# Expert blocks sorted by token count with falling sizes, weights addressed by a register, and GpSimd products in halves, in an RWKV-5 + mixture-of-experts kernel

## The chip, the cores and the metric

The kernel runs on one core of a Trainium2 chip. The metric is device time of one execution in microseconds. The engines are TensorE (PE in the profile; its weight loads are PEld), VectorE (DVE), ScalarE (ACT), GpSimd (POOL) and SyncE (SP, which here only issues DMAs).

## The reference

Attention with a decaying state (batch 4, 8 heads, 768 tokens, head size 48) gives x; then each token goes through one of eight experts with a hidden size of 1024:

```python
for t in range(S):
    cur = einsum('bhd,bhe->bhde', u[None] * k_t, v_t)
    y[:, :, t] = einsum('bhd,bhde->bhe', r_t, state + cur)
    state = w[None, :, :, None] * state + einsum('bhd,bhe->bhde', k_t, v_t)
...
logits = einsum('bsd,de->bse', x, w_gate)              # x: 4 x 768 x 384
local_gate = sigmoid(x @ w_local)
for b in range(B):
    prev_e = -1
    for s in range(S):
        fresh_e = argmax(logits[b, s])
        e = fresh_e if s == 0 or local_gate[b, s] < 0.5 else prev_e
        prev_e = e
        p = softmax(logits[b, s])
        out[b, s] = p[e] * (relu(x[b, s] @ w1[e]) @ w2[e])
```

How many tokens an expert gets depends on the data. Counted from the reference with its fixed inputs, experts 0 to 7 get 417, 353, 336, 448, 376, 390, 329 and 423 tokens; of those, batches 0 and 1 send 212 to expert 0 and 171 to expert 1.

## The kernel before

**Attention** works on 16 items (a batch and a pair of heads), six chunks of 128 tokens each, as matmuls with decays folded into r and k. `Attention.run` writes the order of all engines out by hand; nothing is scheduled. In iteration n, SP loads item n+2 (`load`), GpSimd makes three products for item n+1 (`scale`: ke, pd, rw, L154 to L157), VectorE makes kw (`added`, L165), masks the scores (am, L212), multiplies own (L197) and adds up xT (L237). The two score matmuls of an iteration take PSUM banks from a ring of three, and the second gets its bank when xT of the item before has been written. After each batch its logits are made (lp, L259, and lq, L267) and x is written to DRAM.

**Router.** `Router` finds each token's expert and its slot (the place among the expert's tokens) by scans and one-hot matmuls, in two groups: batches 0 and 1 inside the attention's iterations 9 to 16 (`g` in `run` is 8), batches 2 and 3 inside the first expert units (`Experts.routing`, by step s). Slots are turned into a table of token numbers and of gates by `summed` (matmuls of one-hots), `copied` and `turned`. Each expert owns four columns of 128 slots.

**Experts.** Work runs in ten units of `Experts.run`. Units 0 and 1 take the first 192 slots (HEAD) of experts 0 and 1, which need only batches 0 and 1; units 2 and 3 take the rest of these two experts, 256 slots each; units 4 to 9 take experts 2 to 7 with 448 slots each (CAP). A unit gathers its tokens' rows of x with indirect DMAs from GpSimd's queue (`gather`), transposes them on PE (`turn`, etp, copied to exT), and makes eight times h = w1 x, a ReLU on ScalarE (hT) and y += w2 hT. `drain` copies y to yT, and `send`, one a step during the next unit, transposes 128 slots (otp), multiplies by the gate (yo) and scatters the rows to the output. Slots that hold no token are computed too. Weights of the next expert (w1t, w2t, 1.5 MB each) are fetched by SP into a pool of two buffers, opened when attention's memory has been released. If an expert has more tokens than slots, `over` is above 0 and a branch behind the experts computes everything again in a general way (`general_experts`, 31 blocks of 128).

Of the kernel before, what the change touches and what calls it, by code (L numbers as in the profile page):

```python
# [20 lines left out]
P = 128  # L21
# [13 lines left out]
CAP = 448  # L35
# [6 lines left out]
TAIL = 256  # L42

# [13 lines left out]
class Attention:  # L57
# [9 lines left out]
    def __init__(self, tc, st, rk_d, kv_d, vT_d, x_d, w_t, wp_d, mask, ident, lt):  # L67
# [5 lines left out]
        self.late = st.enter_context(tc.tile_pool(name="late", bufs=2))  # L73
        self.wp = self.late.tile([P, H, 32], F32, name="wp", bufs=1)
        self.sel = self.late.tile([P, E + 1], F32, name="sel", bufs=1)
# [68 lines left out]
    def scale(self, n):  # L144

        nc, t, pw = self.nc, self.items[n], self.pw
        t["ke"] = self.two.tile([P, NCH, 2 * DH], F32, name="ke")
        t["pd"] = self.two.tile([P, NCH, P], F32, name="pd")
        t["rw"] = self.three.tile([P, NCH, P], F32, name="rw")
        hp = t["hp"]  # L150
        if n == 0:
            nc.vector.tensor_mul(t["rw"], t["rT"], spread(pw[:, hp, :P], 1, NCH))
            nc.gpsimd.tensor_mul(t["pd"], t["rT"], t["kT"])
        nc.gpsimd.tensor_mul(t["ke"], t["k"], spread(self.endT[:, hp].rearrange("p i d -> p (i d)"), 1, NCH))  # L154
        if n:
            nc.gpsimd.tensor_mul(t["pd"], t["rT"], t["kT"])  # L156
            nc.gpsimd.tensor_mul(t["rw"], t["rT"], spread(pw[:, hp, :P], 1, NCH))  # L157
# [67 lines left out]
    def before(self, n):  # L225
        nc, t = self.nc, self.items[n]
        if t["hp"] == 0:
            self.xTs[t["b"]] = self.late.tile([P, H, C2 * P], F32, name="xT")
            self.xs[t["b"]] = self.late.tile([P, NCH, D], F32, name="x")
# [23 lines left out]
    def logits(self, b, banks):  # L253
        nc, xT = self.nc, self.xTs[b]
        self.lTs[b] = lT = self.late.tile([P, 2, C2 * P], F32, name="lT", bufs=1)
# [15 lines left out]
    def run(self, router):  # L271
# [9 lines left out]
        for n in range(M + 1):  # L281
            if n + 2 < M:
                self.load(n + 2)
            if n == 0:
# [9 lines left out]
            if n == M:  # L294
                router.turned(0, pair("tb")[0])
                router.head()
# [118 lines left out]
class Router:  # L415
# [7 lines left out]

    def __init__(self, tc, once, mpp, lt, mask, ident, gid, sid, gate, over):
# [4 lines left out]
        self.tok = once.tile([P, E * ST], F32, name="tok")  # L429
        self.tok1 = once.tile([P, E * ST], F32, name="tok1")  # L430
        self.gid0 = once.tile([P, EARLY * ST], I32, name="gid0")
        self.g = []
        for i, (b0, nb) in enumerate(GROUPS):
            c = nb * NCH
            g = dict(b0=b0, nb=nb, nc=c, z=slice(b0 * NCH, b0 * NCH + c))
            for name, shape, dt in (
                    ("mx", [P, c], F32), ("eq", [P, c, E], F32), ("k", [P, c], F32), ("key", [P, c], F32),
                    ("run", [c, P], F32), ("rn", [P, c], F32), ("go", [P, c], F32), ("inc", [P, c + 1], F32),
                    ("ei", [P, 3, c], I32), ("oh", [P, E, c], F32),
                    ("ext", [P, E, c + 1], F32), ("exc", [P, E, c + 1], F32), ("seg", [P, E, c + 1], F32),  # L440
                    ("pos", [P, E, c], F32), ("far", [P, EARLY, c], F32), ("r", [P, c], F32), ("si", [P, 3, c], I32),
                    ("eqv", [P, c, E * ST], F32), ("val", [P, c, E * ST], F32), ("ohq", [P, c, P], F32),
                    ("ex", [P, c, E], F32), ("sm", [P, c], F32), ("pe", [P, c], F32)):
                g[name] = once.tile(shape, dt, name=f"{name}{i}")
            self.g.append(g)
# [13 lines left out]
    def constants(self, part):  # L459
# [12 lines left out]
        else:  # L472
            for g in self.g:
                nc.gpsimd.memset(g["seg"], 1.0)
                nc.gpsimd.memset(g["seg"][:, :, 0:1], 0.0)

                nc.gpsimd.memset(g["go"], 1.0)
                nc.gpsimd.memset(g["go"].rearrange("p (b c) -> p b c", c=NCH)[:, :, NCH - 1:], 0.0)
                nc.gpsimd.memset(g["inc"][:, 0:1], 0.0)
            nc.gpsimd.memset(self.g[0]["ext"][:, :, 0:1], 0.0)  # L480

            self.lim = self.tl("lim", [1, E])
            nc.gpsimd.memset(self.lim, float(CAP))
            nc.gpsimd.memset(self.lim[:, :EARLY], float(CAP + TAIL - HEAD))

# [19 lines left out]
    def runs(self, i):  # L505

        g = self.g[i]
        self.nc.vector.tensor_tensor_scan(g["run"], g["kp"], g["seg"][:g["nc"], 0, 0:1].to_broadcast([g["nc"], P]), 0.0,
# [13 lines left out]
    def one_hot(self, i):  # L522

        nc, g = self.nc, self.g[i]
        nc.vector.tensor_tensor_scan(g["inc"][:, 1:], g["bc"], g["go"], 0.0, Alu.max, Alu.mult)
# [14 lines left out]
    def slots(self, i):  # L540
# [3 lines left out]
        nc.vector.tensor_tensor_scan(g["exc"].rearrange("p e c -> p (e c)"), g["seg"].rearrange("p e c -> p (e c)"),  # L544
                                     g["ext"].rearrange("p e c -> p (e c)"), 0.0, Alu.mult, Alu.add)
        nc.vector.tensor_tensor(g["pos"], g["exc"][:, :, :n], g["rk"].rearrange("p (e c) -> p e c", e=E), op=Alu.add)
        if i == 0:

            nc.vector.tensor_scalar(g["far"], g["pos"][:, :EARLY], float(HEAD), float(TAIL - HEAD), Alu.is_ge, Alu.mult)
            nc.vector.tensor_tensor(g["pos"][:, :EARLY], g["pos"][:, :EARLY], g["far"], op=Alu.add)  # L550
        nc.vector.tensor_tensor(g["pos"], g["pos"], g["oh"], op=Alu.mult)
        nc.vector.tensor_reduce(g["r"], g["pos"].rearrange("p e c -> p c e"), axis=AX.X, op=Alu.add)
# [3 lines left out]
        end = g["exc"][:, :, n:]  # L556
        if i == 0:
            base = self.g[1]["ext"][:, :, 0:1]
            nc.vector.tensor_copy(base, end)
            nc.vector.tensor_scalar(base[:, :EARLY], end[:, :EARLY], float(TAIL - HEAD), float(TAIL), Alu.add, Alu.max)  # L560
        else:
            big = self.tl("big", [1, E])
            nc.vector.tensor_tensor(big, end[0:1, :, 0], self.lim, op=Alu.is_gt)
            nc.vector.tensor_reduce(self.over, big, axis=AX.X, op=Alu.add)

    def columns(self, i):
# [3 lines left out]
        nc.vector.tensor_tensor(g["val"], g["eqv"], spread(self.t1[:, g["z"]], 2, E * ST), op=Alu.mult)  # L570
# [20 lines left out]
    def turned(self, what, bank):  # L591

        nc = self.nc
        nc.tensor.transpose(bank[:, :P], self.rows, self.ident)
        out = self.gate if what else self.tok
        nc.vector.tensor_reduce(out, bank[:, :P].rearrange("q (k j) -> q j k", k=4), axis=AX.X, op=Alu.add)

    def head(self):

        self.nc.vector.tensor_scalar(self.gid0, self.tok[:, :EARLY * ST], -1.0, 0.0, Alu.add, Alu.max)  # L600

    def tokens(self):
        nc = self.nc
        nc.vector.tensor_scalar(self.tok1, self.tok, -1.0, 0.0, Alu.add, Alu.max)
        nc.vector.tensor_scalar(self.gid, self.tok1, float(N - 1), None, Alu.min)
# [13 lines left out]

    def ends(self):  # L620
        nc = self.nc
        none = self.tl("none", [P, E * ST])
        nc.vector.tensor_scalar(none, self.tok, 0.0, float(4 * N), Alu.is_equal, Alu.mult)
        nc.vector.scalar_tensor_tensor(self.sid, self.tok, -1.0, none, Alu.add, Alu.add)
# [168 lines left out]
class Experts:  # L793
# [4 lines left out]
    def __init__(self, tc, st, x_d, w1, w2, out, ident, router):  # L798
        self.tc, self.nc = tc, tc.nc
        self.x_d, self.w1, self.w2, self.ident, self.router = x_d, w1, w2, ident, router  # L800

        self.outs = dram_disjoint_views(out, E * ST)

        def unit(e, first, slots):
# [358 lines left out]
```

## Time and profile before

| | |
|---|---|
| median of 3 timed runs | 475.46 us (474.88 to 477.63) |
| profiled execution | 480.13 us, span 478.3 us |
| attention | 0 to about 136 us |
| units 0 and 1 (192 slots) | about 144 to 183 us |
| units 2 and 3 (256 slots) | about 183 to 229 us |
| units 4 to 9 (448 slots) | about 229 to 459 us |
| mean granted TensorE clock | 0.968 |

A profile row of the timeline gives start, duration, engine, line, operation, output and inputs, shape, and in brackets the idle time of the engine before it with what ended it. Rows that follow each other without a gap are merged (x6 is six instructions, whose time is given together). A float32 matmul shows as two passes.

### The profile page before, as it was taken

What the parts mean: (1) busy time and instruction counts of PE and PEld (TensorE: products, weight loads), DVE (VectorE), ACT (ScalarE), POOL (GpSimd) and SP (SyncE); (2) the same over time, 40 slices, a digit from 0 to 9 for tenths busy, and PEclk for the clock granted to TensorE, in tenths of its full rate; (3) what the DMA queues carried; (4) which work ended last, traced back from release to release, by engine and by line L of the source; (5) the groups of instructions that cost most, each with busy time, mean ns of one, the idle gap of its engine ahead of it and who ended that gap; (6) DMA issues with size and microseconds to landing.
All of it is one profiled execution on the core that took longest, in us unless ns stands there. A gap on an engine that the chain in (4) does not pass through costs nothing.

```text
span 478.3 us, 8704 instructions
## 1 busy us (share of the span) xinstructions
PE 444.1 (93%) x3721; PEld 306.8 (64%) x3721; DVE 159.8 (33%) x266; ACT 78.5 (16%) x226; POOL 147.7 (31%) x142
## 2 busy tenths in 40 slices
PE   3999899969979999999999999999999999999970
PEld 1898897958859989888555555555555555555530
DVE  7597687894811622121101111111111121111030
ACT  2123223213212211111111111110111010110100
POOL 4989785744030021522021014024014002001020
PEclk9999999988978999999999999999999999999995
DMA  8978979752437120271710712612431250001001
GB/s 305 382 244 290 343 276 308 271 191 102 168 147 297 68 66 19 82 299 58 281 40 25 265 44 58 229 68 74 152 153 45 89 220 34 0 2 43 0 33 29
DMA packets 16911, 69.34 MB, mean 145 GB/s; under 512 B 2877, under 2 KB 6263, under 8 KB 14816
## 3 DMA queue, kind: packets, MB, share of 16 engines
q1 hardware_dynamic: 9600, 50.60, 29.1%
q0 software_dynamic: 3840, 10.23, 6.5%
q10 hardware_dynamic: 3424, 7.86, 4.3%
q8 instruction: 31, 0.51, 0.4%
q14 instruction: 16, 0.13, 0.1%
HBM read 59.25 MB, written 10.22 MB: 145 GB/s over the span
## 4 chain that ended last, share of the span: by engine, by line
issue 53%; PE 29%; POOL 11%; DVE 2%; another core or an unknown queue 1%; DMA 1%; POOLq 0%; ACT 0%; SPq 0%; DVEq 0%; ACTq 0%
POOL out_dram L896 6%; PE sc L210 6%; POOL xg L846 5%; PE yp L221 4%; PE tp L246 3%; PE T L172 3%; PE dp L193 2%; PE h L867 2%; PE y L878 2%; PE T L181 2%; PE yp L234 2%; PE lq L267 1%; PE lp L259 1%; DMA rk<-in_rk_dram 1%
## 5 line engine op out<-in xcount | busy, mean ns | idle before, releaser
L878 PE MATMUL y<-hT,w2t 128*128 128x448 f32 (+2 forms) x480 | 158.5, 466 | 1.1 <-ACT hT L870 1.1
L867 PE MATMUL h<-exT,w1t 128*128 128x448 f32 (+2 forms) x480 | 158.4, 470 | 0.0
L867 PEld LDWEIGHTS h<-exT,w1t 128*128 128x128 f32 x480 | 88.8, 194 | 50.2 <-issue 47.8
L878 PEld LDWEIGHTS y<-hT,w2t 128*128 128x128 f32 x480 | 86.3, 191 | 47.4 <-issue 43.5
L896 POOL DMA_INDIRECT out_dram<-yo,sid x32 | 31.4, 982 | 214.4 <-DVE yo L895 213.8
L870 ACT ACTIVATE hT<-h 128x448 f32<-128x448 f32 (+2 forms) x80 | 37.4, 468 | 241.8 <-PE h L867 241.8
L895 DVE TENSOR_SCALAR yo<-otp,gate 128x384 f32<-128x384 f32 (+1 forms) x32 | 19.5, 615 | 107.9 <-PE otp L893 107.7
L846 POOL DMA_INDIRECT xg<-x_d,gid x32 | 32.2, 1005 | 70.2 <-DVE ex L610 29.5
L860 DVE COPY exT<-etp 128x384 f32<-128x384 f32 (+1 forms) x32 | 16.2, 507 | 112.7 <-PE etp L859 112.7
L210 PE MATMUL sc<-rw,kw 48*64 48x128 f32 x768 | 32.9, 287 | 3.9 <-DVE xT L237 3.9
L154 POOL TENSOR_TENSOR ke<-kv,endT 128x576 f32<-128x576 f32 x16 | 24.6, 1539 | 20.4 <-PE T L172 9.5
L156 POOL TENSOR_TENSOR pd<-rk 128x768 f32<-128x768 f32 x15 | 28.0, 1868 | 9.0 <-issue 6.1
L210 PEld LDWEIGHTS sc<-rw,kw 48*64 48x64 f32 x768 | 28.1, 141 | 4.0 <-DVE xT L237 4.0
L212 DVE TENSOR_TENSOR am<-sc,mask 128x768 f32<-128x768 f32 x32 | 29.1, 948 | 2.9 <-PE sc L210 2.9
L181 PE MATMUL T<-S,wd 48*64 48x64 f32 x256 | 27.6, 236 | 0.6 <-ACT S L174 0.3
L157 POOL TENSOR_TENSOR rw<-rk,pw 128x768 f32<-128x768 f32 x15 | 26.6, 1772 | 0.0
L221 PE MATMUL yp<-am,kv 128*64 128x128 f32 x384 | 25.7, 284 | 0.8 <-issue 0.8
L181 PEld LDWEIGHTS T<-S,wd 48*64 48x64 f32 x256 | 22.0, 140 | 5.1 <-issue 2.7
L183 ACT COPY S<-T 128x64 f32<-128x64 f32 x64 | 13.6, 212 | 67.2 <-PE T L181 67.2
L237 DVE TENSOR_TENSOR xT<-yp,own 128x768 f32<-128x768 f32 x16 | 15.3, 956 | 24.4 <-PE yp L234 24.3
L221 PEld LDWEIGHTS yp<-am,kv 128*64 128x64 f32 x384 | 22.0, 143 | 1.3 <-issue 1.2
L165 DVE TENSOR_TENSOR kw<-rk,inv 128x768 f32<-128x768 f32 x16 | 22.6, 1410 | 0.1
(136 smaller groups left out, 300.4 us busy)
## 6 DMA issues: line engine op xcount, KB each, us to landing
rk<-in_rk_dram SPq DMA_DIRECT2D x16, 768.0 KB, 5.0
w1t<-in_w_dram SPq DMA_DIRECT2D x7, 1536.0 KB, 6.8
w2t<-in_w_dram SPq DMA_DIRECT2D x7, 1536.0 KB, 8.2
kv<-in_kv_dram SPq DMA_DIRECT2D x16, 584.0 KB, 6.1
vT<-in_vT_dram SPq DMA_DIRECT2D x16, 384.0 KB, 5.4
x_d<-x ACTq DMA_DIRECT2D x4, 1152.0 KB, 7.9
w1t<-in_w_dram ACTq DMA_DIRECT2D x1, 1536.0 KB, 7.8
w2t<-in_w_dram ACTq DMA_DIRECT2D x1, 1536.0 KB, 11.1
```

What stands on the lines that cost most here:

```text
L154: nc.gpsimd.tensor_mul(t["ke"], t["k"], spread(self.endT[:, hp].rearrange("p i d -> p (i d)"), 1, NCH))
L156: nc.gpsimd.tensor_mul(t["pd"], t["rT"], t["kT"])
L157: nc.gpsimd.tensor_mul(t["rw"], t["rT"], spread(pw[:, hp, :P], 1, NCH))
L181: nc.tensor.matmul(t["T"][h * DP:(h + 1) * DP, c], lhsT=self.wd[q, t["hp"]], rhs=t["S"][q, c - 1], start=False, stop=True, skip_group_chec ...
L210: nc.tensor.matmul(sc[z, h, c * P:(c + 1) * P], lhsT=t["kw"][q, 3 * g + c, z], rhs=t["rw"][q, 3 * g + c], start=True, stop=True)
L212: nc.vector.tensor_mul(t["am"][:, g], sc[:, :, :3 * P].rearrange("p h (c t) -> p h c t", t=P), spread(spread(self.mask, 1, 3), 1, 2))
L221: nc.tensor.matmul(t["y"][p * DP:(p + 1) * DP, h, c2 * P:(c2 + 1) * P], lhsT=t["v"][:, (2 * c + h) * DH:(2 * c + h) * DH + DP], rhs=t["am" ...
L846: self.nc.gpsimd.indirect_dma_start(out=xg[:n], out_offset=None, in_=self.x_d[:rows], in_offset=bass.IndirectOffsetOnAxis(ap=gid[:n, c:c + ...
L867: nc.tensor.matmul(h[:, :n], lhsT=u["w1"][:, m, kk, :], rhs=u["xT"][:, kk, :], start=(kk == 0), stop=(kk == DK - 1))
L870: nc.scalar.activation(u[m], h[:, :n], Act.Relu)
L878: nc.tensor.matmul(u["y"][d][:, :n], lhsT=u["w2"][:, m, d * P:(d + 1) * P], rhs=u[m], start=(m == 0), stop=(m == FK - 1))
L896: nc.gpsimd.indirect_dma_start(out=self.outs[c], out_offset=bass.IndirectOffsetOnAxis(ap=r.sid[:n, c:c + 1], axis=0), in_=yo[:n], in_offse ...
```

## The change

The last eight units are no longer tied to an expert. When all tokens are counted, VectorE ranks the experts by the tokens that are still to be done, the most first (`Router.blocks`, seven small operations at step 4, between pos and r), and unit 2 + b takes the expert of rank b with a fixed number of slots, `BLOCKS[b]`. The tail of experts 0 and 1 becomes such a block like the others, and their weights are fetched a second time. The expert's number is read by SP from `order` into a register, which addresses the weights. The tables of tokens and gates are permuted from experts to blocks by a product with the one-hot `of` and a sum (`rest`); units 0 and 1 have small tables of their own (`heads`). `exceeded` compares each expert's rest with its block's size.

```diff
-CAP = 448
+BLOCKS = (448, 424, 392, 376, 352, 336, 232, 192)
...
-        nc.gpsimd.tensor_mul(t["ke"], t["k"], spread(self.endT[:, hp].rearrange("p i d -> p (i d)"), 1, NCH))
+        for z in (slice(0, C2), slice(C2, NCH)):
+            nc.gpsimd.tensor_mul(t["ke"][:, z], t["k"][:, z], spread(self.endT[:, hp].rearrange("p i d -> p (i d)"), 1, C2))
         if n:
-            nc.gpsimd.tensor_mul(t["pd"], t["rT"], t["kT"])
-            nc.gpsimd.tensor_mul(t["rw"], t["rT"], spread(pw[:, hp, :P], 1, NCH))
+            for z in (slice(0, C2), slice(C2, NCH)):
+                nc.gpsimd.tensor_mul(t["pd"][:, z], t["rT"][:, z], t["kT"][:, z])
+            for z in (slice(0, C2), slice(C2, NCH)):
+                nc.gpsimd.tensor_mul(t["rw"][:, z], t["rT"][:, z], spread(pw[:, hp, :P], 1, C2))
...
             if n + 2 < M:
                 self.load(n + 2)
+            elif n + 2 == M:
+                fetch()
...
             if n == g + 4:
+                router.ranks(0)
+            if n == g + 5:
                 router.slots(0)
-            if n == g + 5:
                 router.columns(0)
-            if n in (g + 6, g + 7):
-                router.places(0, n - g - 6)
+            if n == g + 6:
+                router.numbers(0)
+                router.places(0, 0)
+            if n == g + 7:
+                router.places(0, 1)
...
+    def blocks(self):
+        nc, end = self.nc, self.g[1]["exc"][:, :, self.g[1]["nc"]]
...
+        nc.vector.scalar_tensor_tensor(self.c8, end, float(E), self.tie, Alu.mult, Alu.add)
+        nc.vector.tensor_tensor(gt, spread(self.c8, 1, E), spread(self.c8, 2, E), op=Alu.is_gt)
+        nc.vector.tensor_reduce(rank, gt, axis=AX.X, op=Alu.add)
+        nc.vector.tensor_tensor(self.of, spread(rank, 1, E), spread(self.ie, 2, E), op=Alu.is_equal)
...
+    def rest(self, table, out):
+        nc.vector.tensor_reduce(self.tok[:, EARLY:], table[:, EARLY:], axis=AX.X, op=Alu.add)
+        nc.vector.tensor_reduce(self.tok[:, :EARLY, :2], table[:, :EARLY, TAIL // P:], axis=AX.X, op=Alu.add)
...
+        nc.vector.tensor_tensor(self.by, spread(self.tok.rearrange("p e j -> p j e"), 1, E), spread(self.of, 2, ST), op=Alu.mult)
+        nc.vector.tensor_reduce(out.rearrange("p (b j) -> p b j", b=E), self.by, axis=AX.X, op=Alu.add)
...
-        self.units += [unit(e, TAIL // P, CAP - HEAD) for e in range(EARLY)]
-        self.units += [unit(e, 0, CAP) for e in range(EARLY, E)]
+        self.units += [unit(None, n, b * ST, r.gid, r.sid, r.gate) for b, n in enumerate(BLOCKS)]
...
+        self.wps = [st.enter_context(tc.tile_pool(name="wp0", bufs=1, reuse_waits="tile"))]
...
+            e = self.nc.values_load(self.router.order[0:1, i - EARLY:i - EARLY + 1], engines=[ET.SP], min_val=0, max_val=E - 1,
...
+            w1, w2 = [w[bass.ds(e, 1)].rearrange("o p x -> (o p) x") for w in (self.w1, self.w2)]
...
         if s == 4:
             r.counts(1, [bank("rk1"), bank("tt1")])
+            r.ranks(1)
+            r.blocks()
             r.slots(1)
             r.columns(1)
+            r.numbers(1)
...
+        if s == 5:
+            self.fetch(EARLY, self.nc.sync)
...
-        att.run(router)
+        att.run(router, lambda: ex.fetch(0, nc.sync))
         ex.open(st)
-        ex.fetch(0, nc.sync)
```

Three places show what moves. The first is VectorE in attention's iteration 12 (`n == g + 4`), from the product kw to xT; before, it held the whole slot arithmetic (exc, pos and far are ranks, r and si are slots):

```order
L165 TENSOR_TENSOR kw<-rk_160,inv 128x768
L544 SCALAR_TENSOR_TENSOR exc_100<-seg_101,ext_99 128x104
L546 TENSOR_TENSOR pos_102<-exc_100,rk 128x96
L549 TENSOR_SCALAR far_103<-pos_102 128x24
L550 TENSOR_TENSOR pos_102<-pos_102,far_103 128x24
L551 TENSOR_TENSOR pos_102<-pos_102,oh_98 128x96
L552 TENSOR_REDUCE r_104<-pos_102 128x12
L553 SCALAR_TENSOR_TENSOR si_105<-r_104,ei_97 128x12
L554 TENSOR_SCALAR si_105<-si_105 128x12
L555 TENSOR_SCALAR si_105<-si_105 128x12
L559 COPY ext_122<-exc_100 128x8
L560 TENSOR_SCALAR ext_122<-exc_100 128x2
```

After, on the same engine, r and si stand one iteration later, behind the next xT, own, am and kw:

```order
L585 TENSOR_TENSOR pos_104<-pos_104,oh_102 128x96
L243 TENSOR_TENSOR xT<-yp,own 128x768
L203 TENSOR_TENSOR own<-dp,vT_145 128x768
L218 TENSOR_TENSOR am<-sc,mask 128x768 x2
L171 TENSOR_TENSOR kw<-rk_140,inv 128x768
L614 TENSOR_REDUCE r_106<-pos_104 128x12
L615 SCALAR_TENSOR_TENSOR si_107<-r_106,ei_101 128x12
L616 TENSOR_SCALAR si_107<-si_107 128x12
L617 TENSOR_SCALAR si_107<-si_107 128x12
L622 TENSOR_TENSOR eqv_108<-si_107,ij_i 128x384
```

Four operations left the row ahead of xT. The second place is VectorE at the start of unit 1 (step 8), where the gather's token numbers (gid) are made ahead of the softmax (ex); before:

```order
L596 TENSOR_REDUCE tok<-tb_2307 128x32
L604 TENSOR_SCALAR tok_87<-tok 128x32
L605 TENSOR_SCALAR gid<-tok_87 128x32
L610 TENSOR_TENSOR ex_109<-lt,mx_89 128x96
L612 TENSOR_REDUCE sm_110<-ex_109 128x12
```

and after, with the permutation to blocks (by is the product with the one-hot):

```order
L659 TENSOR_REDUCE tok<-tb_2393 128x24
L660 TENSOR_REDUCE tok<-tb_2393 128x2x2
L663 TENSOR_TENSOR by<-tok,of 128x256
L664 TENSOR_REDUCE tok_2394<-by 128x32
L670 TENSOR_SCALAR at_2401<-tok_2394 128x32
L671 TENSOR_SCALAR gid<-at_2401 128x32
L700 TENSOR_TENSOR ex_111<-lt,mx_94 128x96
```

Three operations more stand ahead of ex, on which ScalarE's exponential and the ReLU behind it wait. The third place is SP's queue, from the last load of attention (vT) on; after the change:

```order
L142 DMA vT_145<-in_vT_dram 128x768
L924 DMA w1t<-in_w_dram 128x3072
L926 DMA w2t<-in_w_dram 128x3072
L920 TENSOR_LOAD order
L924 ISA
L924 DMA w1t<-in_w_dram 128x3072
L926 ISA
L926 DMA w2t<-in_w_dram 128x3072
```

The first pair goes to memory of its own and is not held back by attention's buffers any more; each later pair has a register load and two preparing instructions ahead of it. Unit 1's pair is still issued by ScalarE.

More of the change, by code (lines that the diff above doesn't have):

```diff
@@ L432, in __init__ @@
+        self.order = once.tile([1, E], I32, name="order")
         self.g = []
         for i, (b0, nb) in enumerate(GROUPS):
[L434 to L444, printed above, removed]
```

207 lines of the change are left out of this document (130 added, 77 removed).

## The prediction

> **What bounds the kernel now.** I read the page first, then the table by windows, the timeline of each stage, and the chain of waits for the attention stage.
>
> ```profile
> PE 444.1 (93%) x3721; PEld 306.8 (64%) x3721; DVE 159.8 (33%) x266; ACT 78.5 (16%) x226; POOL 147.7 (31%) x142
> ```
>
> TensorE is busy for 93% of the span, so a gain must shorten what PE does or one of its waits. The timeline shows what expert matmuls cost; a row holds three matmuls of two passes each.
>
> ```profile
> 170.46 1.14 PE L867 MATMUL h<-exT,w1t 128*128 128x192 f32 x6
> 171.43 1.14 PE L878 MATMUL y<-hT,w2t 128*128 128x192 f32 x6
> ...
> 243.38 2.42 PE L878 MATMUL y<-hT,w2t 128*128 128x448 f32 x6
> 245.63 2.42 PE L867 MATMUL h<-exT,w1t 128*128 128x448 f32 x6
> ...
> 262.61 0.33 SPq L831 DMA_DIRECT2D w1t<-in_w_dram  x1
> 301.52 0.33 SPq L831 DMA_DIRECT2D w1t<-in_w_dram  x1
> ```
>
> From start to start six passes take 0.97 us with 192 slots and 2.25 us with 448: 1.28 us for 256 slots, 5.0 ns a slot, with almost nothing fixed (192 x 5.0 ns is 0.96). A unit has 16 such groups, so a slot costs 80 ns. Two fetches stand 38.91 us apart, the length of one 448 unit: 16 x 2.25 = 36.0, and 2.9 for eight passes of three transposes, 0.36 each. From 183 us on PE is bound by slots alone.
>
> Before that there are two holes, each followed by a low granted clock. In the windows table the columns are busy us (instructions) of PE, PEld, DVE, ACT, POOL, then clock and DMA.
>
> ```profile
> 20.00:30.00 10.00, 10.00 (x238) 9.08 (x236) 7.95 (x9) 2.40 (x10) 10.00 (x7) 1.00 0.69 220
> 60.00:70.00 10.00, 10.00 (x244) 9.24 (x245) 7.86 (x9) 3.06 (x12) 8.24 (x6) 1.00 0.71 253
> 100.00:110.00 10.00, 6.15 (x79) 3.71 (x72) 8.72 (x12) 1.28 (x4) 3.02 (x2) 0.67 0.34 126
> 130.00:145.00 15.00, 12.07 (x115) 9.28 (x112) 4.22 (x13) 2.83 (x8) 4.18 (x4) 0.75 0.39 141
> ```
>
> **Blocks: the main term.** Slots over all units fall from 2 x 192 + 2 x 256 + 6 x 448 = 3584 to 2 x 192 + 2752 = 3136. 448 x 80 ns = **-35.8 us**. Units stay ten, so nothing fixed is added. Chunk passes inside the stream: gathers turned 30 before, 27 after; sends 28 before, 27 after (the last unit's are in the tail): 4 x 0.36 = **-1.4**. The partly filled chunks are bounded by nothing and a whole pass; I count whole ones.
>
> **Tail.** The last unit has 192 slots instead of 448.
>
> ```profile
> 183.47 0.68 DVE L886 COPY yT<-y 128x192 f32<-128x192 f32 x2
> 460.01 1.31 DVE L886 COPY yT<-y 128x448 f32<-128x448 f32 x2 [16.75 <-PE y L878]
> 462.64 0.98 POOL L896 DMA_INDIRECT out_dram<-yo,sid  x1 [18.18 <-DVE yo L895]
> 466.51 0.91 POOL L896 DMA_INDIRECT out_dram<-yo,sid  x1 [0.30 <-issue]
> ```
>
> Four sends stand 1.29 us apart and two remain: -2.6; the two drain copies on VectorE fall from 1.31 to 0.68: -0.6. **-3.2**.
>
> **Attention.** Its beat is the write of xT.
>
> ```profile
> 34.15 0.96 DVE L237 TENSOR_TENSOR xT<-yp,own 128x768 f32<-128x768 f32 x1 [0.42 <-PE yp L234]
> 40.23 0.96 DVE L237 TENSOR_TENSOR xT<-yp,own 128x768 f32<-128x768 f32 x1 [1.10 <-PE yp L234]
> 49.33 0.96 DVE L237 TENSOR_TENSOR xT<-yp,own 128x768 f32<-128x768 f32 x1 [3.76 <-PE yp L234]
> ...
> 92.56 0.95 DVE L237 TENSOR_TENSOR xT<-yp,own 128x768 f32<-128x768 f32 x1
> 99.42 0.32 DVE L552 TENSOR_REDUCE r<-pos 128x12 f32<-128x96 f32 x1
> 99.77 1.77 DVE L553 SCALAR_TENSOR_TENSOR si<-r,ei 128x12 int32<-128x12 f32 x1
> 103.31 0.95 DVE L237 TENSOR_TENSOR xT<-yp,own 128x768 f32<-128x768 f32 x1
> 114.88 0.96 DVE L237 TENSOR_TENSOR xT<-yp,own 128x768 f32<-128x768 f32 x1 [6.06 <-PE yp L234]
> ...
> 99.72 1.80 POOL L156 TENSOR_TENSOR pd<-rk 128x768 f32<-128x768 f32 x1 [0.89 <-POOL ke L154]
> ...
> 104.32 1.55 PE L210 MATMUL sc<-rw,kw 48*64 48x128 f32 x24 [3.85 <-DVE xT L237]
> ```
>
> A plain iteration takes 6.08 us, one with logits 9.10. The iteration with the slot arithmetic takes 10.75 (4.67 too long) and the next, with logits at the low clock, 11.57 (2.47 too long). From 99.42 to 103.04 VectorE is at r and si, and a 12-element operation lasts 1.77 us because GpSimd's pd runs beside it: both end within 0.03 us of each other. The change moves r and si behind the next kw, into the iteration whose xT has 3.76 us of idle time before it (row 49.33). So 3.6 us of stall go, and with them, likely, the low clock behind it (2.47). What is late next: about 1 us stays before xT (exc, far, pos). The product of numbers, now in one iteration with half of ohq, adds some 0.3 us there. **-5.8**, with ends -2.5 (clock stays low) and -7.1.
>
> GpSimd in halves: each of its three products an iteration becomes two instructions. What the cut costs isn't shown; I bound it by what a 768-element product holds beyond its elements: 1.80 us against 1.40 for the 576 of ke leaves some 0.15 at most, three times an iteration, so 0 to 0.4. At 8.24 us busy in 10, or 5.0 of 6.08, GpSimd has 1.1 us an iteration spare beside PE's work, so I cost it at 0; at 20 to 30 us it has none (10.00), and there every further 0.1 would be paid: see the rivals. Eight more small constants at about 48 us stand in the same slack.
>
> **First weights.** Fetched after the last load (about 105 us) instead of 120 and 129, when attention's memory came free. Nothing waited for them; the gain can only be at the passage to the experts.
>
> ```profile
> 128.88 0.33 SPq L833 DMA_DIRECT2D w2t<-in_w_dram  x1
> 131.83 1.26 POOL L846 DMA_INDIRECT xg<-x_d,gid  x1 [12.59 <-DVE gid L600]
> 135.02 0.85 PE L259 MATMUL lp<-xT,wp 64*32 64x384 f32 x8 [0.33 <-DVE xT L237]
> 137.79 0.86 ACT L262 COPY lT<-lp 128x384 f32<-128x384 f32 x2 [6.17 <-remote]
> 138.32 1.41 PE L859 MATMUL etp<-ident,xg 128*128 128x128 f32 x6 [2.46 <-ACT lT L262]
> 139.88 2.73 PE L267 MATMUL lq<-sel,lT 128*128 128x9 f32 x12
> 143.77 4.05 PE L867 MATMUL h<-exT,w1t 128*128 128x192 f32 x12
> ...
> 74.32 1.44 PE lq L267 x12
> ```
>
> PE is idle for 2.46 us although lp had ended at 135.87; ScalarE's copy started 1.9 us after that, for a reason the trace calls remote. In the same microseconds the 1.5 MB of w2t and the head gathers are under way. Behind the hole the clock is low: lq 2.73 instead of 1.44, twelve passes of h 4.05 instead of 1.94, and about 1.0 in the transposes between: 4.4 us. If the gathers no longer meet w2t, 1.6 of the hole and the 4.4 go; if the unknown releaser is something else, nothing goes. Between 0 and 6.0 I take **-5.0**, nearer to the rows of earlier batches, where lT follows lp at once.
>
> **What is added in units 0 and 1.**
>
> ```profile
> 165.42 0.29 DVE L596 TENSOR_REDUCE tok<-tb 128x32 f32<-128x128 f32 x1 [0.72 <-PE tb L594]
> 168.82 0.28 ACT L611 ACTIVATE ex<-ex 128x96 f32<-128x96 f32 x1 [2.21 <-DVE ex L610]
> 169.38 1.24 PE L878 MATMUL y<-hT,w2t 128*128 128x192 f32 x6 [1.07 <-ACT hT L870]
> 183.60 2.75 PE L867 MATMUL h<-exT,w1t 128*128 128x256 f32 x12
> ...
> L109 DVE TENSOR_TENSOR pw<-pw 128x256 f32<-128x256 f32 x1 | 0.4, 424 | 0.0
> ```
>
> At the start of unit 1 PE already waits 1.07 us for a ReLU queued on ScalarE behind two exponentials, which wait for VectorE. VectorE now does six rows for the gather's numbers instead of three, among them a product of 128x256 (0.42 by the last row) and its sum (0.29 to 0.6; I take 0.45): +1.1 us, so PE waits 2.2. At step 14 some 13 small rows more, about 2.9 us, stand ahead of two exT copies; the next unit's first h comes 0.7 later through two more transposed chunks, so 0.5 remains (0 to 1.5). At step 4 seven rows (1.3 us) stand before ohq, which had 1.1 us in hand: 0.2. **+1.8**.
>
> **Weights by a register.** The load of the number and a preparing instruction stand on SP ahead of each pair of fetches, which wait anyway for the unit before to release its buffer.
>
> ```profile
> w1t<-in_w_dram SPq DMA_DIRECT2D x7, 1536.0 KB, 6.8
> w2t<-in_w_dram SPq DMA_DIRECT2D x7, 1536.0 KB, 8.2
> ```
>
> The last number is the median us to landing, so a pair lands within 15 us even if one follows the other; the shortest cover is a unit of 192 slots, 15.5 us and its transposes, for unit 2, and w2 is needed later than w1. I cost it at 0; the bound above is a few us once.
>
> **Sum.** -35.8 - 1.4 - 3.2 - 5.8 - 5.0 + 1.8 = -49.4. The profiled execution took 480.13 us (span 478.3 and 1.8 around it): 430.7. The median of the timed runs is 4.67 us lower. If they save it in the low-clock stretches, which go anyway, none of it carries over; otherwise all. Half of it gives **428.4 us**.
>
> **Rivals.**
> - The passage stays as it is: 5 more, about 433. For it: the unnamed releaser. Against: w2t's traffic is gone from there.
> - A new low-clock stretch in unit 1, after the 2.2 us wait: the window of 0.67 above holds some 7 us at half clock, 3.5 to 4.5 more, 432.5. For it: a hole of 2.46 us was followed by the low clock. Against: the 1.07 us wait was not. The Trainium skill ("TensorE: Matmul & The Clock Gate", Part 1) puts the fall behind a whole idle window of about 3.4 us. By that rule this rival would add nothing; the row at 138.32 shows less idle time before a low clock, so I leave the rival its chance.
> - GpSimd becomes the bound in attention. It gives way to kw between two halves: 5.0 us of work, 0.3 for the cuts and up to 0.95 of waiting are 6.25 against 6.08, 0.2 x 14 iterations = 2.4 more, 431. The Trainium skill ("SBUF — State Buffer", Who interferes with whom) says that whichever of the two starts first holds the shared ports for the whole instruction; the ends at 101.5 agree, and by it a half stops VectorE for half as long but can be stopped as often again.
> - Weights come late, where an address from a register costs more than a fixed one: past 15 us a pair, unit 2 waits, then the last units: 5 to 15 more, 438.
> - Slower: a block overflows. Counting the reference's choices, 448, 423, 390, 376, 336, 329, 225 and 182 tokens remain for blocks of 448, 424, 392, 376, 352, 336, 232 and 192. Two fit with nothing to spare. If one token more falls into such an expert on the chip, the branch behind the experts computes everything again in 31 blocks of 128: 31 x 128 x 80 ns = 317 us more, some 745. Against it: expert 3 had exactly 448 of 448 before too, and the page ends without the branch.
>
> **Chances.** Forecast (within 424 to 431.5) 0.58; passage stays 0.16; low clock in unit 1 0.10; GpSimd 0.05; weights 0.06; overflow 0.03; 0.02 for a smaller time than all. The range of 421 to 438 reaches from all gains at their ends (about 422) to two of the small rivals together. About 0.5%, 2.4 us, is what a measurement can tell: every case but overflow is faster by far more. Faster 0.96, same 0.01, slower 0.03.
>
> **What would show it.** After: rows of y with 424, 392, 376, 352, 336, 232 slots, each 5.0 ns a slot; no PE wait for xT over 1.2 us near 100 us; clock 1.00 in that window and at the passage; y waiting for hT some 2.2 us in unit 1; SP's fetches landing before their units. A floor under the small matmuls, a PE wait for DMA at a unit's start, or rows behind the branch would make it wrong.

## The result and the profile after

The changed kernel's median is 428.0 us (425.7 to 431.1, 4 runs) against 475.17 for the kernel before beside it: a ratio of 0.901, 95% interval 0.893 to 0.909. Profiled it took 429.32 us, span 427.4. It was run again on a chip where the kernel before takes 478.55 us: 434.75, a ratio of 0.907 (0.905 to 0.910). The gain is 44 to 47 us.

The page's busy times and two groups of instructions (busy us, mean ns of one | idle us before, and what ended most of it):

```profile
PE 401.2 (94%) x3703; PEld 299.7 (70%) x3703; DVE 155.1 (36%) x282; ACT 75.1 (18%) x226; POOL 154.4 (36%) x190
...
L967 PE MATMUL y<-hT,w2t 128*128 128x192 f32 (+7 forms) x480 | 140.7, 430 | 2.2 <-ACT hT L959 2.2
L956 PE MATMUL h<-exT,w1t 128*128 128x192 f32 (+7 forms) x480 | 140.5, 433 | 0.1
```

TensorE does 43 us less and is as full as before. Of the 960 passes of the expert matmuls only one waits noticeably, one of y in unit 1 (2.2 us); none waits for weights from the register-addressed fetches. The timeline of the changed kernel shows the blocks, six passes a row:

```profile
199.94 2.42 PE L967 MATMUL y<-hT,w2t 128*128 128x448 f32 x6
...
228.44 2.30 PE L967 MATMUL y<-hT,w2t 128*128 128x424 f32 x6
...
255.86 2.14 PE L967 MATMUL y<-hT,w2t 128*128 128x392 f32 x6
...
305.75 2.06 PE L967 MATMUL y<-hT,w2t 128*128 128x376 f32 x6
...
329.70 1.94 PE L967 MATMUL y<-hT,w2t 128*128 128x352 f32 x6
...
352.08 1.86 PE L967 MATMUL y<-hT,w2t 128*128 128x336 f32 x6
...
389.83 1.34 PE L967 MATMUL y<-hT,w2t 128*128 128x232 f32 x6
...
404.25 1.14 PE L967 MATMUL y<-hT,w2t 128*128 128x192 f32 x6
```

From 448 to 192 slots, 1.28 us go for 256 slots: 5.0 ns a slot, without a floor down to 192 slots. Where the time went by stage, from the starts of the xT writes (items counted from 0), of each unit's first h, and the end of the last y; two profiles of each kernel, the second ones (before_again, after_again) both from one chip:

| stage, us | before | before_again | after | after_again |
|---|---|---|---|---|
| start to xT of item 10 | 92.56 | 92.90 | 91.87 | 92.78 |
| two iterations with slot arithmetic and logits | 22.32 | 21.26 | 15.90 | 16.49 |
| three more, to the last xT | 19.12 | 19.10 | 18.76 | 19.31 |
| passage: last xT to first h | 9.77 | 8.68 | 6.71 | 10.15 |
| unit 0 | 20.36 | 20.64 | 20.70 | 19.73 |
| unit 1 | 19.47 | 19.47 | 21.70 | 23.38 |
| units 2 to 9 | 277.06 | 277.07 | 238.53 | 238.53 |
| from the last y to the end | 17.65 | 17.64 | 13.23 | 13.15 |
| span | 478.31 | 476.76 | 427.39 | 433.51 |

The stream repeats to 0.01 us. What differs most between the two profiles of the changed kernel is the passage (3.4 us) and unit 1 (1.7), the two places where TensorE waits; no other stage of either kernel differs by more than 1.1. At the passage the first profile of the changed kernel seemed to show the forecast:

```profile
127.99 1.02 POOL L935 DMA_INDIRECT xg<-x_d,gid  x1 [0.30 <-issue]
128.44 0.86 ACT L268 COPY lT<-lp 128x384 f32<-128x384 f32 x2 [3.60 <-PE lp L265]
...
128.97 0.98 PE L948 MATMUL etp<-ident,xg 128*128 128x128 f32 x6 [0.58 <-ACT lT L268]
...
130.17 1.91 PE L273 MATMUL lq<-sel,lT 128*128 128x9 f32 x12 [0.21 <-DVE exT L949]
...
133.24 4.05 PE L956 MATMUL h<-exT,w1t 128*128 128x192 f32 x12
```

lT follows lp at once and the hole is 0.58 instead of 2.46. Yet lq takes 1.91 where 1.44 was its time in an earlier batch (2.73 at the passage before the change), and h 4.05 as before: a low clock stayed. In unit 1 the wait is the one forecast:

```profile
159.49 0.25 DVE L700 TENSOR_TENSOR ex<-lt,mx 128x96 f32<-128x96 f32 x1
159.78 0.28 ACT L701 ACTIVATE ex<-ex 128x96 f32<-128x96 f32 x1 [2.21 <-DVE ex L700]
159.97 0.53 ACT L959 ACTIVATE hT<-h 128x192 f32<-128x192 f32 x2
...
160.33 1.24 PE L967 MATMUL y<-hT,w2t 128*128 128x192 f32 x6 [2.21 <-ACT hT L959]
```

VectorE feeds the exponential, ScalarE does the ReLU (hT) behind it, and y waits 2.21 us.

### The profile page after: what moved, and what is told of

It reads as the page before. It is cut to its first block, busy times and chain, and to the rows that moved or that the text cites. A ratio compares the mean times of both kernels' runs of the same rounds, so it can differ in the third digit from the quotient of the medians.

```text
span 427.4 us, 8781 instructions
## 1 busy us (share of the span) xinstructions
PE 401.2 (94%) x3703; PEld 299.7 (70%) x3703; DVE 155.1 (36%) x282; ACT 75.1 (18%) x226; POOL 154.4 (36%) x190
## 4 chain that ended last, share of the span: by engine, by line
PE 87%; DVE 5%; DMA 2%; issue 2%; POOL 1%; SPq 1%; ACT 0%; DVEq 0%; ACTq 0%
PE h L956 30%; PE y L967 29%; PE sc L216 5%; PE yp L227 5%; PE tp L252 3%; PE T L178 2%; PE otp L982 2%; PE etp L948 2%; PE dp L199 2%; DMA kv<-in_kv_dram 2%; PE yp L240 2%; PE lp L265 1%; PE lq L273 1%; PE T L187 1%; DVE am L218 1%
## 5 line engine op out<-in xcount | busy, mean ns | idle before, releaser
L967 PE MATMUL y<-hT,w2t 128*128 128x192 f32 (+7 forms) x480 | 140.7, 430 | 2.2 <-ACT hT L959 2.2
L956 PE MATMUL h<-exT,w1t 128*128 128x192 f32 (+7 forms) x480 | 140.5, 433 | 0.1
L985 POOL DMA_INDIRECT out_dram<-yo,sid x29 | 28.7, 989 | 194.2 <-DVE yo L984 193.9
L959 ACT ACTIVATE hT<-h 128x192 f32<-128x192 f32 (+7 forms) x80 | 34.4, 431 | 211.9 <-PE h L956 211.9
L949 DVE COPY exT<-etp 128x384 f32<-128x384 f32 (+7 forms) x29 | 14.1, 493 | 103.9 <-PE etp L948 103.9
L984 DVE TENSOR_SCALAR yo<-otp,gate 128x384 f32<-128x384 f32 (+7 forms) x29 | 17.8, 615 | 91.5 <-PE otp L982 91.5
L935 POOL DMA_INDIRECT xg<-x_d,gid x29 | 29.6, 1022 | 52.5 <-DVE ex L700 27.1
L161 POOL TENSOR_TENSOR pd<-rk 128x384 f32<-128x384 f32 x30 | 32.3, 1098 | 6.2 <-issue 5.2
L163 POOL TENSOR_TENSOR rw<-rk,pw 128x384 f32<-128x384 f32 x30 | 33.1, 1123 | 0.0
L158 POOL TENSOR_TENSOR ke<-kv,endT 128x288 f32<-128x288 f32 x32 | 25.5, 818 | 5.3 <-DMA kv<-in_kv_dram 2.4
## 6 DMA issues: line engine op xcount, KB each, us to landing
x_d<-x ACTq DMA_DIRECT2D x4, 1152.0 KB, 10.6
```

Of the source, the lines that this page charges most:

```text
L158: nc.gpsimd.tensor_mul(t["ke"][:, z], t["k"][:, z], spread(self.endT[:, hp].rearrange("p i d -> p (i d)"), 1, C2))
L161: nc.gpsimd.tensor_mul(t["pd"][:, z], t["rT"][:, z], t["kT"][:, z])
L163: nc.gpsimd.tensor_mul(t["rw"][:, z], t["rT"][:, z], spread(pw[:, hp, :P], 1, C2))
L935: self.nc.gpsimd.indirect_dma_start(out=xg[:n], out_offset=None, in_=self.x_d[:rows], in_offset=bass.IndirectOffsetOnAxis(ap=u["gid"][:n, ...
L956: nc.tensor.matmul(h[:, :n], lhsT=u["w1"][:, m, kk, :], rhs=u["xT"][:, kk, :], start=(kk == 0), stop=(kk == DK - 1))
L959: nc.scalar.activation(u[m], h[:, :n], Act.Relu)
```

## The experiments

They went to four chips: e_flat, e_whole, e_back and e_late to one (the kernel before takes 475.6 there), b_split, e_w2, e_fill and e_fill_gates to a second (480.3), after_again, before_again and e_gates to a third (478.6), e_gather to a fourth (475.2). So medians are compared within a group, or as ratios to before; stages are compared across all.

**e_flat: the slots back.**

```diff
-BLOCKS = (448, 424, 392, 376, 352, 336, 232, 192)
+BLOCKS = (448, 448, 448, 448, 448, 448, 256, 256)
```

> The changed kernel with blocks of 448 six times and 256 twice: 3584 slots again instead of 3136, still sorted by falling count, ten units, the last one of 256. If slots alone make the gain of the stream: 448 x 80 ns = 35.8, three chunks more in and out at 0.36 a pass = 2.2, the last drain 0.2: 38.2 us more than the changed kernel, about 467.5 profiled, ratio to before about 0.98. Rival, the gain comes from the order or from small blocks at the end (a shorter drain, weights that come in time): under 30 us more, and the rows of 448 slots show something other than 2.25 us for six passes.

Measured: 470.1 us, ratio 0.986 (0.978 to 0.994); profiled 471.05. Units 2 to 9 take 276.98 us, 38.45 more than in the changed kernel, where 35.8 + 2.2 = 38.0 were expected. Sorting, the register and the small blocks at the end bring nothing by themselves: the slots are the whole gain of the stream. The profile is 3.5 us above the 467.5 expected, mostly because the tail took 16.02 us, 2.8 more than in after. The longer drain is none of it: the last send starts 3.06 us behind the last y, against 3.04, and the rest lies after that send.

**e_whole: GpSimd's products in one piece.**

```diff
-        for z in (slice(0, C2), slice(C2, NCH)):
-            nc.gpsimd.tensor_mul(t["ke"][:, z], t["k"][:, z], ...
+        nc.gpsimd.tensor_mul(t["ke"], t["k"], spread(self.endT[:, hp].rearrange("p i d -> p (i d)"), 1, NCH))
...
```

> The changed kernel with GpSimd's products in one piece again (ke, pd, rw of 768 or 576 elements). Theory A, the halves cost GpSimd time that nothing hides while it is busy all the time: the windows from 20 to 60 us get shorter, the iteration with the small constants falls from 10.56 back to about 9.1 to 9.5, 0.7 to 1.5 us less in all, and the iteration of the slot arithmetic stays near 7.0. Theory B, the halves are what keeps VectorE from standing behind a product: xT near 99 and 108 us comes later, a PE wait for xT of 1 us or more is back, and the time is 1 to 4 us longer. If neither: within 0.7 us.

Measured: 431.76, ratio 0.907 (0.900 to 0.914). Neither theory: the iteration of the slot arithmetic takes 7.14 us with whole products (6.96 with halves), the one behind it 8.85 (8.94), and TensorE waits 0.2 for xT in both. The iteration with the constants took 11.36 here, 1.7 of it by a low clock; with halves it took 9.1 to 10.6 in the nine profiles whose clock stayed high there. The 10.56 of the first profile was one execution, not a bound of GpSimd. The halves by themselves are worth nothing that these runs can tell.

**e_back: r and si back in the iteration of the ranks, halves kept.**

```diff
             if n == g + 4:
                 router.ranks(0)
-            if n == g + 5:
                 router.slots(0)
+            if n == g + 5:
                 router.columns(0)
```

> The changed kernel with r and si back in the iteration of the ranks, halves kept. Theory A, the place of r and si made the gain in attention: PE waits for xT by 2 to 4 us near 99 us, a low granted clock behind it, 3 to 6 us longer. Theory B, the halves alone make it (si now stands behind half a product, some 0.7 to 1.1 us less): PE waits under 1.2 us, clock 1.00, under 1.5 us longer.

The place of r and si in e_back's timeline:

```profile
98.81 0.32 DVE L614 TENSOR_REDUCE r<-pos 128x12 f32<-128x96 f32 x1
99.01 1.94 POOL L161 TENSOR_TENSOR pd<-rk 128x384 f32<-128x384 f32 x2 [0.72 <-POOL ke L158]
99.17 0.86 DVE L615 SCALAR_TENSOR_TENSOR si<-r,ei 128x12 int32<-128x12 f32 x1
100.06 0.92 DVE L616 TENSOR_SCALAR si<-si 128x12 int32<-128x12 int32 x1
...
100.97 0.94 DVE L243 TENSOR_TENSOR xT<-yp,own 128x768 f32<-128x768 f32 x1
...
102.06 0.89 PE L216 MATMUL sc<-rw,kw 48*64 48x128 f32 x24 [2.30 <-DVE xT L243]
```

Two 12-element operations take 0.86 and 0.92 us, each about as long as half a product beside it. In the kernel before they took 1.77 (the row of si in the prediction) and 1.47:

```profile
101.58 1.47 DVE L554 TENSOR_SCALAR si<-si 128x12 int32<-128x12 int32 x1
```

TensorE waits 2.30 for xT (3.85 before the change), and a low clock follows (102.8 to 106.3). The two iterations take 9.12 + 10.50 = 19.62 us against 15.90: 3.7 lost, as theory A had it. Its four runs spread from 427.7 to 434.3, and no ratio with an interval came of them. Halves do cut a stall of this sort, here by 1.5 us; once r and si stand elsewhere, almost nothing is left to cut (in the other changed kernels TensorE waits 0.7 us for xT there at most).

**b_split: the kernel before with that one part of the change.** The four operations on r and si in `slots`, and with them the two small ones on ext behind them, become a function that is called one iteration later, ahead of `columns`; the products stay whole. (The change itself leaves the two on ext where they were.)

> The kernel before with one part of the change alone: r and si go from the iteration of the ranks to the next one, ahead of the columns; GpSimd's products stay whole. Theory A, the place is what counts: xT near 103 us comes 3.5 us earlier (an iteration of about 7.1 instead of 10.75), PE waits under 0.5 us for it, no low clock near 105 us, 4 to 6 us less than before. Theory B, whole products and the place together are needed: VectorE still stands behind a product, 1 us or more of PE wait stays, under 3 us less.

Measured: 473.61 against 480.27 before, ratio 0.989 (0.984 to 0.994). The two iterations take 6.75 + 8.85 = 15.60 us instead of 22.32 or 21.26, TensorE has no wait for xT there, and no low clock follows. Theory A: the place alone makes attention's gain, whole products or not.

**e_late: unit 0's weights in memory that attention frees.**

```diff
-        u, wp = self.units[i], self.wps[i % 2]
+        u, wp = self.units[i], self.wps[(i + 1) % 2]
...
-        att.run(router, lambda: ex.fetch(0, nc.sync))
+        att.run(router, lambda: None)
         ex.open(st)
+        ex.fetch(0, nc.sync)
```

> The changed kernel with unit 0's weights in memory that attention frees (fetched after attention, as before) and unit 1's in the memory of their own. Theory A, the weights' transfers at the passage made the hole: lT starts 1.5 to 2 us after lp again, the PE wait before etp is back at about 2.5, the low clock there lasts 10.24 us instead of 6.83, together 2.5 to 4 us longer. Theory B, they had nothing to do with it: the wait stays near 0.6 and the time within 0.7 us.

Measured: 429.27, ratio 0.903 (0.896 to 0.910). The wait before etp stays at 0.6. But SP issued the pair at 111.6 and 118.1 us, the second 8.7 us before xT was written, where the kernel before had 6.1: it landed at 125.2, before lp, so the next run holds it back further.

**e_w2: unit 0's second weights held back until the passage.** `fetch2` is the second half of the fetch, which the full edit splits.

```diff
                 self.chain(n, 3)
+                if n == M - 1:
+                    nc = self.nc
+                    nc.sync.dma_start(out=self.late.tile([P, 4], F32, name="mark"), in_=self.items[n]["S"][:, 3, :4])
+                    fetch2()
...
```

> The changed kernel with unit 0's second weights (1.5 MB) held back on SP's queue, behind a 16-byte copy that waits for ScalarE's fourth state copy of the last item, so that they are issued some 7 us before lp ends, as before the change. Theory A, their transfer made the hole at the passage: lT starts 1.5 to 2 us after lp again, PE waits some 2.5 us before etp, 1.9 us longer, and a low clock behind it in every execution. Theory B, it was something else: the wait stays at 0.6, the time within 0.7 us of the changed kernel.

e_w2's timeline at the passage:

```profile
123.51 0.57 SPq L932 DMA_DIRECT2D w2t<-in_w_dram  x1
...
127.44 0.96 DVE L243 TENSOR_TENSOR xT<-yp,own 128x768 f32<-128x768 f32 x1 [1.69 <-PE yp L240]
...
131.12 0.86 ACT L268 COPY lT<-lp 128x384 f32<-128x384 f32 x2 [5.37 <-remote]
...
131.66 0.94 PE L954 MATMUL etp<-ident,xg 128*128 128x128 f32 x6 [2.35 <-DMA xg<-x_d,gid]
```

432.33 us, ratio 0.901 (0.897 to 0.904). The hole is back, as theory A expected. (The last row names a gather as what came last; etp starts 0.54 us behind lT, as in the other profiles.) But the other kernels of this group show the late lT too, e_fill with the weights fetched 26 us ahead; so the kernel without an edit had to be run once more.

**e_fill and e_fill_gates: work into the hole; the exponentials elsewhere.**

```diff
         att.logits(B - 1, [self.bank("lp") for _ in range(2)])
+        att.turn(B * HP - 1, [self.hps.tile([P, 512], F32, name="h") for _ in range(2)])
...
-            r.gates(0)
-            r.gates(1)
+        if s == 10:
+            r.gates(0)
+        if s == 11:
+            r.gates(1)
```

The first two lines are e_fill; e_fill_gates has all.

> The changed kernel with the last item's transposes (tp) put ahead of the expert transposes (etp), into two banks of the h pool, so that TensorE has work while ScalarE copies lT. The wait of 0.58 goes in every case. Theory A, a window of about 3.4 us with too little work on TensorE is followed by a window at half clock: the window at the passage has 0.86 us idle now and 0.3 then, the low clock at the passage is gone, passage plus unit 0 last some 23.7 instead of 24.2 (without it) or 27.4 (with it). Theory B, the low clock there comes from the small tiles of lp and lq, not from idle time: it stays in the profile.

> The same, and the two exponentials with their sums moved from step 8 to steps 10 and 11 of unit 1, where nothing else is on VectorE. Theory A, the wait of y for hT comes from them and brings a low clock in many executions: unit 1 lasts 19.5 us instead of 21.7 or 23.4 (with a low clock), the wait of 2.2 is gone, the median is 3 to 7 us under the changed kernel's. Theory B, the hold-up is the numbers of the gather ahead of them: at least 1 us of the wait stays.

e_fill: 430.16, ratio 0.896 (0.891 to 0.900). lT begins 2.72 us after xT is written, though tp lies between, so a wait of 1.55 is left before etp, and the low clock stays: passage and unit 0 last 28.56 us. Theory A's number failed; its window had 1.87 us of idle time, not 0.3. e_fill_gates: 427.57, ratio 0.893 (0.889 to 0.896), 2.6 us under e_fill; unit 1 lasts 20.40 us, without a wait for hT and without the low clock that e_fill has there (23.38). Theory A for the exponentials, though unit 1 lasts 0.9 us more than the 19.5 expected, and the gain was put at 3 us or more.

**after_again, before_again, e_gates, on one chip.** The first two are the kernels as they are; e_gates has only the second half of the edit above.

> The changed kernel as it is, once more, beside the kernel before on the same chip. At the passage the copy lT began 0.95 us after VectorE had written xT in five profiles of the changed code and 2.7 to 3.4 us after it in five others. Theory A, it is the kernel (what is under way at the passage): 0.95 here, whatever the chip. Theory B, it is the chip or the execution: 2.7 here where the kernel before, on the same chip, has 2.7 too. Theory C on the clock, a window of 3.41 us in which TensorE idles for about 2 us is followed by one at half clock: the wait of y in unit 1 (2.2 us) is at that bound, so unit 1 lasts 21.7 us where the windows divide the wait, else 23.4.

> The kernel before as it is, once more, for its passage on the same chip. Theory A: lT begins 2.8 us after xT is written, as in its first profile. Theory B: on a chip where the changed kernel has 0.95, this one has 0.95 too, the hole before etp is gone and its span is 2 to 5 us under the first profile's 478.3.

> The changed kernel with the two exponentials and their sums at steps 10 and 11 of unit 1 instead of step 8, and nothing else. Unit 1 lasts 19.5 us in every execution (21.7 or 23.4 before the edit), no low clock there, and the median is 2.2 to 3.9 us under the changed kernel's on the same chip. If the wait only moves to another ReLU: under 1 us.

The passage of the changed kernel, unedited, on this chip:

```profile
128.41 2.03 PE L265 MATMUL lp<-xT,wp 64*32 64x384 f32 x32
128.58 0.96 DVE L243 TENSOR_TENSOR xT<-yp,own 128x768 f32<-128x768 f32 x1 [1.74 <-PE yp L240]
...
133.10 0.86 ACT L268 COPY lT<-lp 128x384 f32<-128x384 f32 x2 [6.25 <-remote]
133.64 0.87 PE L948 MATMUL etp<-ident,xg 128*128 128x128 f32 x6 [3.20 <-ACT lT L268]
```

The same program that had a hole of 0.58 has one of 3.20; before_again has 2.50. The delay of lT behind the end of xT was 0.95 us in every kernel of the first group, 2.7 to 3.4 in the second, 2.9 to 3.6 here. Theory B: it is the chip or the execution, which these runs do not tell apart, and the change does not remove it. e_gates: 431.46 against 434.75, ratio 0.902 (0.899 to 0.904) against 0.907: it beats both kernels. Unit 1 lasts 20.63 us instead of 23.38, with no wait of y. 19.5 was expected; waits of 0.25 us before etp and 0.31 before mp are part of the rest, which was not followed further.

**e_gather: unit 1's gathers held back, with e_gates's edit.** gid1 is a copy of the token numbers that unit 1 gathers by.

```diff
+        self.nc.vector.tensor_copy(self.router.gid1, self.router.gid0)
+        self.gather(1)
         att.token_logits(B - 1, self.bank("lq"))
...
-        for i in range(EARLY):
-            ex.gather(i)
+        ex.gather(0)
```

> The changed kernel with the exponentials at steps 10 and 11, and with unit 1's two gathers held back until unit 0's rows are transposed, so that GpSimd issues two gathers at the passage instead of four. TensorE's report of the end of lp comes 0, 1.8 or 2.6 us late there, chip by chip, and ScalarE's copy lT waits for it. Theory A, the gathers under way delay it: lT begins under 2 us after xT is written also on a chip where the kernel before takes 478 us or more. Theory B, they don't: 2.7 us or more on such a chip. On a chip with 475 us before, 0.95 is expected of both and tells nothing. Unit 1 lasts about 20 us; the gathers held back aren't late (unit 1's first transposes come 15 us later).

It met a chip where the kernel before takes 475.2, and lT came 0.95 us after xT: as said ahead, that tells nothing on the cause. Its time is 426.04, ratio 0.895 (0.891 to 0.899). The profile, 422.71, is the shortest time of all and shows the stages without any low clock before the end: passage 5.82, unit 0 18.38, unit 1 19.45.

## Why the prediction was right, point by point

- **Blocks, chunk passes: right.** Forecast for the stage of units 2 to 9: -35.8, -1.4 and 0.7 more that moves into unit 1, -37.9. Measured -38.5, and e_flat gives 38.45 back.
- **Attention: right.** Forecast -5.8. The two iterations fell by 6.4 in the first profiles and by 4.8 on one chip, and b_split's one edit alone saved 5.7 to 6.7 there. The stall and the low clock behind it went together. GpSimd's halves were costed at 0 for the time, and e_whole agrees.
- **Tail: -3.2 forecast.** From the last y to the end, 17.65 us became 13.23: -4.4. To the last send it is -2.8: two sends fewer at 1.29 us are 2.6 of it, so the shorter drain saved 0.2 and not 0.6. The other 1.6 lies behind the last send, 11.8 us before and 10.2 after, by the row below against the span; e_flat had 13.0 there. What sets it was not tried.

```profile
417.20 0.93 POOL L985 DMA_INDIRECT out_dram<-yo,sid  x1 [0.30 <-DVE over L1180]
```

- **First weights: wrong, the step that failed.** "If the gathers no longer meet w2t, 1.6 of the hole and the 4.4 go; if the unknown releaser is something else, nothing goes." I took -5.0. The first profile showed -2.7 for passage and unit 0 together; on one chip, before_again and after_again show +0.6. So the term is nothing there, and the rival "the passage stays as it is" held: lT comes as late without w2t's traffic as with it. The argument from earlier batches was weak. Their lT follows lp within 0.11 us in all fourteen profiles, on the chips with the late passage too, so they differ from it in more than the traffic; and the word remote said that the trace has no instruction for the releaser. What releases lT stays open.
- **Units 0 and 1: the wait right, its consequence not.** y waits 2.21 us (2.2 forecast), 1.1 more than before, and unit 1 grew by 2.2, of which 0.7 is the two more chunks that it transposes. But the rival to which I gave 0.10, a low clock behind that wait, came in seven of the eight profiles that have the wait; the first profile is the exception. Its price was 1.7 us (21.70 to 23.38), not 3.5 to 4.5: one window at half clock, not two.
- **GpSimd the bound, weights late, a block that overflows: no.** SP issues unit 2's pair at 150.87 and 154.14 us and a pair takes 7.0 and 8.2 us to land by the page's medians, while unit 2's first h comes at 175.64; no block is computed again. GpSimd is busy for 10.00 of 10 us from 60 to 70 us and TensorE too; with whole products, in e_whole (the second row), GpSimd has 7.71:

```profile
60.00:70.00 10.00, 10.00 (x247) 9.24 (x245) 6.70 (x9) 2.66 (x11) 10.00 (x12) 1.00 0.76 272
60.00:70.00 10.00, 10.00 (x236) 9.07 (x237) 7.86 (x8) 2.89 (x11) 7.71 (x5) 1.00 0.79 285
...
100.00:110.00 10.00, 10.00 (x215) 8.38 (x215) 7.40 (x12) 2.76 (x11) 5.99 (x8) 1.00 0.97 354
```

(Windows tables, the first and the last row of the changed kernel: busy us and instructions of PE, PEld, DVE, ACT, POOL, then clock and DMA. The last row is the stage that had 6.15 us of PE at a clock of 0.67.) So the halves cost no time but were not free: by the page's groups the three products took 79.2 us in all before and 90.9 after, 0.7 us an item, more than the 0 to 0.4 that the prediction allowed for the cuts (how much of it is waiting for VectorE is not known), and the 1.1 us an iteration that it counted as spare is gone where GpSimd is at 10.00.

- **The total.** Forecast -49.4 by profiles, measured -50.8 (480.13 to 429.32). In this pair the 2.1 us missing at the passage and in unit 0 were more than made up by 1.2 in the tail, 1.0 in attention, 0.7 at the start and 0.6 in the stream. But the changed kernel's profile had drawn the passage well, and unit 1 too: on one chip it is -43.0 by profiles (478.49 to 435.45) and -43.8 by medians. With the passage at 0 and a low clock in unit 1 the forecast's own sum is -42.7. So that 428.4 met 428.0 is in part luck: on that chip a term was not there and a rival was, and its 434.75 lies outside the 424 to 431.5 of the forecast, near the 433 of the rival. The step from the profile to the median was the same mistake from the other side: the profiled execution of before, 4.67 us above the median, contained the late lT. That this is the difference is argued and not shown, since the timed runs have no trace; but the kernel before takes 475 us on the two chips where lT came at once in the edited kernels, and 478 to 480 on the two where it came late.

**The clock.** In every profile the low stretches after the first 20 us are multiples of 3.41 us on a fixed grid, but for the last, which the end cuts off. How long TensorE idles in one window goes with the clock of the next. Rows as above; first the changed kernel, then after_again:

```profile
127.69:131.10 3.41, 2.55 (x27) 1.51 (x16) 0.82 (x2) 0.86 (x2) 1.96 (x2) 1.00 0.44 122
131.10:137.93 6.83, 6.83 (x27) 6.83 (x27) 1.42 (x7) 1.66 (x5) 0.00 (x0) 0.50 0.49 176
158.41:161.82 3.41, 1.49 (x9) 1.49 (x10) 2.79 (x12) 0.72 (x3) 2.54 (x3) 1.00 0.86 330
161.82:165.24 3.42, 3.42 (x23) 3.42 (x22) 0.25 (x1) 0.66 (x2) 2.41 (x3) 1.00 0.46 143
```

```profile
161.84:165.25 3.41, 1.19 (x7) 0.90 (x7) 2.54 (x12) 0.97 (x4) 2.77 (x3) 1.00 0.96 394
165.25:168.66 3.41, 3.41 (x13) 3.41 (x12) 1.23 (x5) 0.00 (x0) 2.50 (x4) 0.51 0.49 153
```

The wait of y is the same in both. In the first kernel the grid puts 1.92 us of its idle time into one window, and the clock stays; in the second it puts all 2.22 there, and it falls. Where the edge lies differs from execution to execution, and so a wait of 2.2 us costs 2.2 or 3.9. The Trainium skill ("TensorE: Matmul & The Clock Gate", Part 1) has a free-running window of about 3.4 us, and the grid agrees with it; it puts the fall behind a whole idle window, and the rows differ: 1.19 us of work in the window did not save it.

## What to carry to other kernels

Where the stream is bound by slots, fewer slots pay in full: price them from two tile sizes in the trace. A wait on TensorE near 2 us is worth removing for nearly twice its length, since a low clock may follow, depending on where the window's edge lies (2.2 us cost up to 3.9 here); moving two exponentials by two and three steps gave 2.6 and 3.3 us. And a wait whose releaser the profile cannot name should be looked for in a second execution on another chip before a change is credited with it.

## What was unexpected in the hardware

**What goes before a low clock.** Over all fourteen profiles, on the 3.41 us grid from about 20 us on, where the trace's record of the clock begins, and leaving out windows that are low themselves, I added TensorE's idle time and the time of lq, whose matmuls stream 9 columns behind a weight load of 128:

```
idle + lq in a window     windows   next at half clock
2.02 us and more            31          31
1.65 to 2.00                10           6
less                       all others    1 (1.36)
```

Idle time alone does not order them: at the passage 0.86 us was enough in the first row above, with 0.93 us of lq in that window. e_gather's window has as little idle time with 0.29 us of lq in it, and the clock stayed:

```profile
125.98:129.39 3.41, 2.54 (x33) 1.14 (x21) 1.33 (x4) 0.86 (x2) 0.64 (x1) 1.00 0.31 87
129.39:136.20 6.81, 6.81 (x48) 6.52 (x48) 1.84 (x9) 1.99 (x6) 1.96 (x2) 1.00 0.63 207
```

That lq counts as idle is a reading that orders the windows; no run was made to test it alone.

**A late report.** At the passage ScalarE's copy waits only for TensorE's count, and that came with the last lp of the timeline or 1.8 to 2.7 us behind it, alike within 0.7 us for the kernels on one chip. The copies of the three earlier batches come within 0.11 us on the same chips. It is not unit 0's weights (landed 15 us earlier in after_again, and unit 1's are not issued yet), and tp behind lp does not hasten it (e_fill). What delays it stays open: the gathers under way were to be tested, and the run met a chip that does not show it.
